# A state-space layer and a gated feed-forward on one core: a decay tile in place of a third transpose, and per-block bursts

## The chip, the core and the metric

One core of a Trainium2 chip runs the whole kernel. It has TensorE for matrix products (PE; its weight loads are a row of their own, PEld), VectorE (DVE), ScalarE (ACT), GpSimd (POOL) and a queue engine (SP) that issues most of the transfers. The metric is the device time of the program in microseconds, the median over runs. Three runs of the kernel before gave 408.99, 411.08 and 411.17 us.

## The reference

Two layers follow each other. The first is a state-space layer over batch 4, 8 heads, 768 steps, head size 32 and state size 16, in chunks; the second is a root-mean-square norm and a gated feed-forward over 3072 tokens, 256 channels and 1536 hidden units. The three weight matrices come as 64-bit floats.

```python
cum = np.cumsum(la, axis=-1)                       # la: log of a in the chunk
M = (Cc @ Bc^T) * exp(cum_i - cum_j) * causal      # per batch and head
y_intra = M @ xc
y_inter = (Cc @ state) * exp(cum_i)
state = exp(sum(la)) * state + sum_j Bc_j xc_j^T exp(cum_last - cum_j)
...
xn = x / sqrt(mean(x * x) + 1e-6) * rms_g          # x: y as 3072 x 256
g = xn @ w_gate
out = (g * sigmoid(g) * (xn @ w_val)) @ w_out
```

The chunk length is free in the result; the kernel uses its own.

## The kernel before

*Tiling.* Tokens are worked in six blocks of 512 (`TB`). A block has two pairs, a pair two chunks of 128 tokens (`P`); from pair 2 on each chunk is treated as two halves of 64 (`HC`), with a state each. Eight heads with 16 state rows fill 128 partitions; `NQ` is four groups of two heads, each on 32 partitions.

*The state-space part of a pair.* `load` and `load_x` bring B, C and x. `scale` (L478) makes on VectorE Cd = C times exp(cum), and Bd = B times the decay to the end of the half chunk. `turn` (L494) transposes B, C and Cd of one chunk on TensorE into a tile tp; `turned` (L502) copies the transposed B and Cd into the tile T, and `turned_of` (L509) copies the transposed C twice, each time masked to one head of every two. `products_at_once` (L546) is a burst of 32 small products: C B^T for all heads, into four PSUM banks called g. `decayed` and `decayed_one` (L552, L559) multiply them on VectorE by the decays L, in place. `outputs` (L644) is a burst of small products into four banks y: first the state's part (state times transposed Cd), then the intra part (x times the decayed L), and at its end `additions` (L574), the state additions of the next pair. `squares` and `taken_out` (L688, L705) bring y out, and `states` (L589) makes the new states.

The decays L of pairs 4 to 11 are made like this: `row_sums` and `row_store` (L1005, L1011) put sums of logs into the DRAM tile rowd; `spread` (L453) broadcasts them to 64 partitions each; `subtract`, `exponential` (L460, L467) take the token's own sum off, and apply the exponential and the causal mask (on POOL, L471).

*The feed-forward.* `product_gv` (L826) makes gate and value with seven products per group of two tiles of hidden units, and `taken_gv`, `total_gv`, `silu_gv`, `hide_gv` (L848 to L867) combine them on ScalarE and VectorE. `product_o` (L915) and its combinations do the same for the second matrix. Block 0 uses plain products (`products_early`, `products_gv`, `first_projection`), while the 64-bit weights are fetched and converted (`fetch`, `power`, `mantissa`, `weight`).

*Order.* The order of all steps is written out by hand in one string (`order`, L1114). A step such as `2:P.7.1` is product 7 of group 1 of block 2; `2:g.0` is the C B^T burst of the first pair of the block behind it. Each engine gets its instructions in the order of that string and runs them in that order; waits follow from tiles and buffers. Each transfer on SP waits in its place too.

*Buffers touched.* `raw` has three buffers each for B, C and x; `ssd` two for Cd, Bd, T and L. The banks of PSUM: two single ones (tag "one"), pair 2 for g and y, and four for gate and value. Each `bank` call takes one of the two single ones.

Of the kernel before, what the change touches and what calls it, by code (L numbers as in the profile page):

```python
# [9 lines left out]
FP32 = mybir.dt.float32  # L10
# [10 lines left out]
def kernel(  # L21
# [91 lines left out]
    def load(p, queues=(nc.sync, nc.sync)):  # L113
        b, c0 = divmod(2 * p, NC)
        br = raw.tile([P, 2, NH, N], FP32, tag="br", name="br")
        cr = raw.tile([P, 2, NH, N], FP32, tag="cr", name="cr")
        st.setdefault(p, {}).update(B=br, C=cr)
        for i in range(2):
            sl = slice((c0 + i) * P, (c0 + i + 1) * P)
            for dst, src in ((br, B), (cr, C)):  # L120
                queues[i].dma_start(out=dst[:, i], in_=src[b, :, sl, :].rearrange("h s n -> s h n"))

    def load_x(p, queue=nc.sync):
        b, c0 = divmod(2 * p, NC)
        st.setdefault(p, {})["x"] = raw.tile([P, 2, NH, D], FP32, tag="xr", name="xr")
        for i in range(2):
            sl = slice((c0 + i) * P, (c0 + i + 1) * P)
            queue.dma_start(out=st[p]["x"][:, i], in_=x[b, :, sl, :].rearrange("h s n -> s h n"))
# [284 lines left out]
    def pair_tile(g):  # L413
        p = g // 2
        if p not in Ls:
            Ls[p] = ssd.tile([P, 2, NH, P if p < 2 else HC], FP32, tag="L", name="L", bufs=2)
        return Ls[p][:, g % 2]
# [60 lines left out]
    def scale(p):  # L478
# [3 lines left out]
        for name, src, d in (("Cd", "C", to_i), ("Bd", "B", from_j)):  # L482
# [11 lines left out]
    def turn(p, i, parts=3):  # L494

        s = st[p]
        ps["t", p, i] = tp = bank("tp", (P, parts, P))
        for k, src in enumerate((s["B"], s["C"], s.get("Cd"))[0:parts]):
# [3 lines left out]
    def turned(p, i, copy):  # L502
        tp = ps["t", p, i]
        if tp.shape[1] == 3:
            copy(out=transposed(p)[:, i, 0::3], in_=tp[:, 0::2])
        else:
            copy(out=transposed(p)[:, i, 0], in_=tp[:, 0])

    def turned_of(p, i, t, scaled):  # L509

        scaled(transposed(p)[:, i, 1 + t], ps["t", p, i][:, 1], tmask[:, t:t + 1])
# [11 lines left out]
    def product(p, todo):  # L523
        T = st[p]["T"]
        for i in range(2):
            for q, g in todo:
# [8 lines left out]
                for u in halves:  # L535
                    nc.tensor.matmul(  # L536
                        out=g[u, P * i:P * i + P].rearrange("p (t m) -> p t m", t=2),
                        lhsT=T[r, i, 0, u], rhs=T[r, i, 1:3, u], start=(i == 0), stop=True,
# [7 lines left out]
    def products_at_once(p, g):  # L546
# [3 lines left out]
        product(p, [(0, g[:, 0]), (1, g[:, 1]), (2, g2), (3, g3)])  # L550

# [92 lines left out]
    def outputs(p, y):  # L644

        if p < 2:
            return first_outputs(p, y)
        s = st[p]
        ps["y pair", p] = y
        y = [y[:, 0], y[:, 1], bank("y2", (P, 512)), bank("y3", (P, 512))]  # L650
        ps["y", p] = y
        first = (2 * p) % NC == 0
        opened = set()

        def product_y(k, u, i, rows, **operands):
            nc.tensor.matmul(out=y[2 * k + u][rows, i * HC:(i + 1) * HC],  # L656
# [4 lines left out]
        for i in range(2):  # L661
            for u in range(2):
                for q in range(NQ):
                    if first and i == 0 and u == 0:
                        continue
                    r, o = slice(32 * q, 32 * q + 32), 64 * (q % 2)
                    S = state[2 * (2 * p + i) + u - 1]
                    product_y(q // 2, u, i, slice(o, o + 64),
                              lhsT=S[r].rearrange("p t d -> p (t d)"),
                              rhs=s["T"][r, i, 3, halves[u]], tile_position=(32 * q, o))  # L670
        opened |= {(k, u, o) for k, u, o_ in opened for o in (o_, o_ + 32)}
        for i in range(2):
            for h in range(NH):
                for u in range(2):
                    o = 32 * (h % 4)
                    product_y(h // 4, u, i, slice(o, o + 32), lhsT=s["x"][halves[u], i, h],
                              rhs=Ls[p][halves[u], i, h], tile_position=(HC * u, o))
        if 2 <= p < NPAIR - 1:
            additions(p + 1, [y[u][:, P:2 * P].rearrange("p (i t d) -> p i t d", i=2, t=2)
                              for u in range(2)])  # L680
        del st[p], Ls[p]

    def parts_of_y(p):
        y = ps["y", p]
        return [(0, slice(0, 2), ps["y pair", p][:, :, 0:P])] + [
            (1, slice(u, u + 1), y[2 + u][:, 0:P].unsqueeze(1)) for u in range(2)]

    def squares(p):  # L688
# [3 lines left out]
        tk = slice(half * 256, half * 256 + 256)  # L692
# [5 lines left out]
        sq2 = nrm.tile([P, 2, 2, 2, HC], FP32, tag="sq2", name="sq2", bufs=1)  # L698
        for k, us, y in parts_of_y(p):
            nc.scalar.activation(out=sq2[:, k, :, us].rearrange("p i u m -> p u i m"),  # L700
                                 in_=y.rearrange("p u (i m) -> p u i m", i=2), func=AF.Square)
        s2 = sq2.rearrange("p k i u m -> p k (i u m)")
        nc.gpsimd.tensor_tensor(out=sqs[blk][:, tk], in0=s2[:, 0], in1=s2[:, 1], op=ALU.add)

    def taken_out(p, copy):  # L705
# [3 lines left out]
        tk = slice(half * 256, half * 256 + 256)  # L709
# [5 lines left out]
        for k, us, y in parts_of_y(p):  # L715
            copy(out=yts[blk][:, k, tk].rearrange("p (i u m) -> p u i m", i=2, u=2)[:, us],
                 in_=y.rearrange("p u (i m) -> p u i m", i=2))
# [287 lines left out]
    def row_sums(k):  # L1005

        ps["row", k] = r_ps = bank("r_ps", (P, P))
        nc.tensor.matmul(out=r_ps, lhsT=laf[:, 2 * k * BH:(2 * k + 4) * BH], rhs=mid,
                         start=True, stop=True)

    def row_store(k):  # L1011
        c = 2 * k
        r_sb = nrm.tile([P, P], FP32, tag="r_sb", name="r_sb", bufs=2)
        nc.vector.tensor_copy(out=r_sb, in_=ps.pop(("row", k)))
        nc.sync.dma_start(out=rowd[:, c * BH:(c + 4) * BH].rearrange("u r m -> r u m"),
                          in_=r_sb.rearrange("r (u m) -> r u m", u=2))

# [14 lines left out]
    rowv = rowd.rearrange("u r m -> u (r m)")  # L1032
    def by_scalar(out, in_, scale):
        ac.activation(out=out, in_=in_, func=AF.Copy, scale=scale)

    def by_vector(out, in_, scale):
# [10 lines left out]
        "scale": scale, "turn": lambda p, i: turn(p, i, 3 if p > 1 else 2),  # L1047
        "T": lambda p, i: turned(p, i, ac.copy if p else dv.tensor_copy),
        "Tt": lambda p, i, t: turned_of(p, i, t, by_scalar if p else by_vector),
# [5 lines left out]
        "y": lambda p: outputs(p, take("y", ("y", p))),  # L1055
# [16 lines left out]
        "row": row_sums, "rowout": row_store,  # L1072
# [15 lines left out]
    def of_chunk(n, fn):  # L1088
# [9 lines left out]
        "turn": of_pair(1, turn), "T": of_pair(1, lambda p, i: turned(p, i, ac.copy)),  # L1098
        "Tt": of_pair(1, lambda p, i, t: turned_of(p, i, t, by_scalar)),
        "scale": of_pair(1, scale),  # L1100
        "g": of_pair(1, lambda p: products_at_once(p, pair_of_banks("g", 2))),
        "L": of_pair(1, lambda p: decayed(p, 0)),
        "L1": of_pair(1, decayed_one),
        "A": of_pair(1, additions), "S": of_pair(1, states),
        "y": of_pair(1, lambda p: outputs(p, pair_of_banks("y", 2))),
        "sq": of_pair(1, squares), "yt": of_pair(1, lambda p: taken_out(p, ac.copy)),
# [9 lines left out]
        0:gcol 0:never 0:after 0:fetch.2 0:mid 0:ident16 0:whole16 0:fetch.3 0:idle.7 0:mask.0.0/1  # L1116
        0:mask.0.1/0 0:hmask 0:part 0:part2 0:fetch.4 0:head 0:mids 0:fetch.5 0:bc.2 0:x.2 0:fetch.6
        0:aT 0:la0 0:log4.0.4 0:fetch.7 0:log 0:mask.1.1/2 0:log4.4.2 0:log4.6.2 0:sel 0:upto2
        0:after2 0:whole 0:r.0 0:tmask 0:parts.0 0:middles 0:c*2 0:turn.0.1 0:T.0.1 0:cx 0:kinks
        0:eps 0:Tt.0.1.0 0:d 0:dx 0:fetch.8 0:Tt.0.1.1 0:sums.0.1 0:exp.0.1 0:turn.0.0 0:Tt.0.0.0  # L1120
        0:T.0.0 0:Tt.0.0.1 0:scale.1 0:cc 0:sums.0.0 0:exp.0.0 0:mean 0:turn.1.0 0:never16 0:g.0.1/0
        0:L.0.1 0:turn.1.1 0:bc.3 0:T.1.1 0:Tt.1.0.1 0:Tt.1.1.1 0:Tt.1.0.0 0:T.1.0 0:Tt.1.1.0
        0:fetch.9 0:sums.1.1 0:exp.1.1 0:g.0.0/1 0:scale.0 0:last.0 0:Tl.0 0:L.0.0 0:pow.0 0:man.0
        0:A.0 0:S.0 0:bc.4 0:row.1 0:rowout.1 0:man.1 0:wt.0 0:g.1.1/0 0:A.1 0:S.1 0:last.1 0:pow.1
        0:L.1.1 0:Tl.1 0:pow.2 0:mask.1.0/2 0:sums.1.0 0:exp.1.0 0:row.0 0:g.1.0/1 0:mask.3/0
        0:pow.5 0:man.5 0:fetch.10 0:r.1 0:y.0/2 0:sq.0 0:pow.3 0:L.1.0 0:y.1/1 0:sq.1 0:wt.1
        0:scale.2 0:rowout.0 0:man.2 0:pow.6 0:yt.0 0:ydone.0 0:turn.2.0 0:early.0.0/2 0:parts.1
        0:sums.3 0:exp.3 0:ms.0 0:rs.0 0:wt.2 0:pow.4 0:yt.1 0:ydone.1 0:early.0.1 0:mask.2/0
        0:sums.2 0:turn.2.1 0:man.3 0:wt.5 0:wt.3 0:early.1.0/1 0:early.1.1 0:man.4 0:fetch.11
        0:man.6 0:fetch.14 0:scale.3 0:exp.2 0:pow.7 0:xn.0 0:wt.6 0:T.2.0 0:T.2.1 0:Tt.2.1.0  # L1130
        0:Tt.2.1.1 0:Tt.2.0.0 0:Tt.2.0.1 0:table.0 0:x.3 0:wt.4 0:gate.2/0 0:man.8 0:man.7
# [186 lines left out]
```

## Time and profile before

| | us |
|---|---|
| median of the three runs | 411.08 |
| the profiled execution, its own time | 409.49 |
| its span | 407.4 |
| last chain piece on TensorE ends, then a sum and a store of the result | 404.69 |

| stage (us of the span) | what runs |
|---|---|
| 0 to 26 | start: masks, sums of logs, pairs 0 and 1 |
| 26 to 94 | block 0's feed-forward, conversion of the weights, pairs 2 and 3 |
| 94 to 147 | block 1, pairs 4 and 5 |
| 147 to 390 | blocks 2 to 5, pairs 6 to 11 until 331 |
| 390 to 407 | last products of block 5, result out |

| group (line, engine, what) | count | us busy | mean ns |
|---|---|---|---|
| L499 PE, transposes of Cd | 20 | 5.5 | 273 |
| L536 PE, C B^T from pair 2 on | 320 | 6.9 | 280 |
| L656 PE, y from x and L | 640 | 8.6 | 224 |
| L656 PE, y from the state | 296 | 6.6 | 224 |
| L582 PE, state additions in a y burst | 264 | 5.1 | 226 |
| L484 DVE, Cd | 12 | 5.0 | 415 |
| L562 DVE, L by g, 256 columns | 20 | 8.0 | 418 |
| L556 DVE, L by g, 512 columns | 10 | 6.8 | 681 |
| L1034 ACT, masked copies of C | 44 | 14.0 | 379 |
| L505 ACT, copies of B and Cd | 20 | 7.4 | 372 |
| L703 POOL, sum of the squares | 10 | 7.7 | 766 |
| spread, rowd to L, 128 KB each | 32 | | 3.2 us to landing |
| row sums to rowd, 64 KB each | 2 | | 2.3 us to landing |

How to read it: busy time of a group is the time in which at least one of its instructions runs, so that overlapping small products have a busy time far below count times mean. A product in 32-bit floats is two records. What matters for the end is the distance between starts on TensorE, not the duration of a record: two full products of 256 columns start 216 ns apart, and last 381.

### The profile page before, as it was taken

The page shows a single profiled execution, that of the slowest core. Times are in us where ns is not written, and L with a number is a line of the kernel's source. Part 1 is how long each engine was busy: PE and PEld are TensorE (multiplying, and loading weights), DVE is VectorE, ACT ScalarE, POOL GpSimd, SP SyncE. Part 2 cuts the span into 40 slices and gives each one's busy share as a digit, 9 for nine tenths or more (in the row PEclk, how much of TensorE's full clock was granted, in tenths as well). Part 3 has the DMA queues.
Part 4 walks back from the last instruction along what each step waited for, and adds up shares of the span by engine and source line. Part 5 has one row for each costly group of instructions (what it writes and reads, how often), then busy time and mean ns, then how long its engine had stood idle before and what let it go on. Part 6 is the DMA issues. An engine that isn't in the chain of part 4 may idle for free.

```text
span 407.4 us, 9550 instructions
## 1 busy us (share of the span) xinstructions
PE 399.9 (98%) x3867; PEld 340.4 (84%) x3867; DVE 303.7 (75%) x698; ACT 231.9 (57%) x506; POOL 37.5 (9%) x61
## 2 busy tenths in 40 slices
PE   8999999999899999999999999999999999999997
PEld 4566577888688899888899988899988899988997
DVE  5999999898976787856799278779455777265863
ACT  3899989795556445664584355534566442453500
POOL 4010000003200001300023000001300000000000
PEclk9999999999999999999999999999999999999999
DMA  9998937400401171302080501020300000100001
GB/s 112 231 213 173 266 118 209 53 0 5 75 0 28 29 126 39 44 1 55 20 131 8 79 2 53 2 80 2 77 2 0 2 4 0 53 1 2 0 2 52
DMA packets 87371, 23.91 MB, mean 59 GB/s; under 512 B 76800, under 2 KB 81152, under 8 KB 87328
## 3 DMA queue, kind: packets, MB, share of 16 engines
q1 hardware_dynamic: 83168, 23.05, 26.9%
q10 hardware_dynamic: 4160, 0.26, 0.8%
q8 instruction: 30, 0.49, 0.5%
q14 instruction: 13, 0.11, 0.1%
HBM read 20.02 MB, written 3.28 MB: 57 GB/s over the span
## 4 chain that ended last, share of the span: by engine, by line
PE 90%; DVE 4%; ACT 3%; DMA 1%; issue 1%; SPq 0%; ACTq 0%
PE gate L844 27%; PE o L934 22%; PE val L844 20%; PE o L876 4%; PE gate L760 3%; PE y L656 3%; PE tp L499 2%; PE gate L770 2%; PE g L536 1%; PE ms L725 1%; DVE sw L814 1%; DVE s L907 1%; DMA L<-rowd 1%; PE e L422 1%; ACT e L183 1%
## 5 line engine op out<-in xcount | busy, mean ns | idle before, releaser
L856 DVE TENSOR_TENSOR c<-val,p 128x512 f32<-128x512 f32 x99 | 67.6, 688 | 46.3 <-PE val L844 27.5
L850 ACT COPY p<-gate 128x512 f32<-128x512 f32 x99 | 57.4, 586 | 52.4 <-PE gate L844 49.2
L844 PE MATMUL gate<-tx,sw 128*128 128x256 f32 x264 | 65.5, 381 | 0.0
L865 ACT ACTIVATE c<-c 128x256 f32<-128x256 f32 x99 | 39.9, 417 | 41.8 <-DVE c L856 41.6
L844 PEld LDWEIGHTS gate<-tx,sw 128*128 128x128 f32 x264 | 49.1, 190 | 7.0 <-ACT p L850 0.3
L869 DVE TENSOR_TENSOR h<-c 128x256 f32<-128x256 f32 x99 | 41.4, 433 | 17.4 <-ACT c L865 17.3
L844 PE MATMUL val<-tx,sw 128*128 128x256 f32 x132 | 33.9, 381 | 1.2 <-DVE c L856 1.2
L844 PE MATMUL val<-xn,wgv 128*128 128x256 f32 x132 | 34.1, 380 | 0.0
L844 PE MATMUL gate<-xn,wgv 128*128 128x256 f32 x132 | 34.0, 382 | 0.0
L844 PE MATMUL val<-xn,sw 128*128 128x256 f32 x132 | 33.9, 381 | 0.0
L844 PE MATMUL gate<-tx,wgv 128*128 128x256 f32 x132 | 33.8, 383 | 0.0
L471 POOL TENSOR_SCALAR_AFFINE_SELECT L<-L 64x512 f32<-64x512 f32 x32 | 23.5, 734 | 83.3 <-ACT L L469 72.9
L934 PEld LDWEIGHTS o<-two,s 128*128 128x128 f32 x240 | 28.3, 192 | 1.9 <-issue 1.4
L934 PE MATMUL o<-wo,h 128*128 128x128 f32 x240 | 29.5, 275 | 0.0
L934 PE MATMUL o<-two,s 128*128 128x128 f32 x240 | 29.3, 276 | 0.1
L934 PEld LDWEIGHTS o<-wo,h 128*128 128x128 f32 x240 | 28.4, 192 | 0.7 <-DVE h L869 0.2
L934 PE MATMUL o<-two,h 128*128 128x128 f32 x240 | 28.9, 275 | 0.0
L844 PEld LDWEIGHTS val<-tx,sw 128*128 128x128 f32 x132 | 24.7, 190 | 5.0 <-DVE c L856 1.6
L844 PEld LDWEIGHTS gate<-tx,wgv 128*128 128x128 f32 x132 | 24.4, 190 | 4.2 <-ACT p L850 0.6
L934 PEld LDWEIGHTS o<-two,h 128*128 128x128 f32 x240 | 27.8, 192 | 0.0
L844 PEld LDWEIGHTS val<-xn,wgv 128*128 128x128 f32 x132 | 24.5, 190 | 3.9 <-DVE c L856 0.6
L844 PEld LDWEIGHTS val<-xn,sw 128*128 128x128 f32 x132 | 24.6, 190 | 3.5 <-DVE h L869 0.2
(179 smaller groups left out, 645.9 us busy)
## 6 DMA issues: line engine op xcount, KB each, us to landing
L<-rowd SPq DMA_DIRECT2D x32, 128.0 KB, 3.2
xr<-in_x_dram SPq DMA_DIRECT2D x24, 128.0 KB, 4.2
wr<-in_moe_w_out_dram SPq DMA_DIRECT2D x6, 512.0 KB, 5.0
wr<-in_moe_w_gate_dram SPq DMA_DIRECT2D x5, 512.0 KB, 5.8
wr<-in_moe_w_val_dram SPq DMA_DIRECT2D x5, 512.0 KB, 5.9
out_dram<-ob SPq DMA_DIRECT2D x9, 256.0 KB, 2.2
br<-in_B_dram SPq DMA_DIRECT2D x22, 64.0 KB, 3.8
cr<-in_C_dram SPq DMA_DIRECT2D x22, 64.0 KB, 3.1
```

The lines of the kernel that those rows point to most:

```text
L471: nc.gpsimd.affine_select(out=L[r], in_=L[r], pattern=[[0, NH], [1, HC]], compare_op=ALU.is_ge, fill=0.0, base=0, channel_multiplier=-1)
L499: nc.tensor.transpose(out=tp[:, k], in_=src[:, i].rearrange("p h n -> p (h n)"), identity=ident)
L656: nc.tensor.matmul(out=y[2 * k + u][rows, i * HC:(i + 1) * HC], start=(k, u, rows.start) not in opened, stop=True, skip_group_check=True, ...
L760: nc.tensor.matmul(out=gv[:, k], lhsT=w[:, t, fs], rhs=xns[0][:, t], start=(t == 0), stop=(t == 1))
L770: nc.tensor.matmul(out=gv[:, k, tk], lhsT=w[:, t, fs], rhs=yts[0][:, t, tk], start=(s == 0 and t == 0), stop=(t == 1), skip_group_check=True)
L844: nc.tensor.matmul(out=dst[:, half[w]], lhsT=lhsT, rhs=rhs, start=(k in (1, 2, 5) and w == 0), stop=True, skip_group_check=True)
L850: nc.scalar.copy(out=t, in_=Xs[j])
L856: nc.vector.tensor_tensor(out=t, in0=Zs[j], in1=a, op=ALU.add)
L865: nc.scalar.activation(out=u, in_=src[:, half[0]], func=AF.Silu)
L869: nc.vector.tensor_tensor(out=hidden_tile(blk, j)[:, c // 10 - 1, c % 10 - 1], in0=u, in1=src[:, half[1]], op=ALU.mult)
L876: nc.tensor.matmul(out=o, lhsT=hs_[blk, f // 2][:, f % 2, k // 2, (k % 2) * P:(k % 2 + 1) * P], rhs=wo[:, f], start=opens, stop=(f == NF - ...
L934: nc.tensor.matmul(out=o[t] if apart else o[:, t * P:(t + 1) * P], lhsT=lhsT[:, t], rhs=rhs, start=(k in (1, 2, 4, 5) and j == 0 and (apar ...
```

## The change

- The transposes of Cd go for pairs 2 to 11 (`turn` makes B and C alone). `scale` makes only Bd there. In place of the transposed Cd, T gets the transposed C times a decay tile dT (`turned_decayed`, on VectorE out of PSUM).
- dT holds exp(cum) for each head, on that head's 16 partitions. `row_sums` gets a second product, with the matrix `upto`; `row_decays` applies the exponential and stores the rows into a new DRAM tile rowe; `spread_decays` broadcasts a pair's rows into dT (in the buffers of Cd).
- `turn`, `turned`, `turned_of` treat a pair at once, not a chunk at once, from pair 2 on.
- Blocks 2 to 5 (pairs 4 to 11): one burst of C B^T for both pairs, into g of full width (`products_of_block`); L is one tile for the block and multiplied in three instructions (`decayed_block`); one burst of outputs for both pairs, with the additions of both pairs of the next block at its end; squares and copies at double width, and the first square goes straight into sq.
- Buffers: B and C two instead of three, x four instead of three, r_sb three instead of two.
- The order is written anew throughout, the start included (places of fetches, loads, conversions, fillers).

```diff
-        br = raw.tile([P, 2, NH, N], FP32, tag="br", name="br")
+        br = raw.tile([P, 2, NH, N], FP32, tag="br", name="br", bufs=2)
...
+            Ls["of", p // 2] = L = ssd.tile([P, 4, NH, HC], FP32, tag="L", name="L", bufs=2)
...
-        for name, src, d in (("Cd", "C", to_i), ("Bd", "B", from_j)):
+        for name, src, d in (("Cd", "C", to_i), ("Bd", "B", from_j))[0 if p < 2 else 1:]:
...
+    def spread_decays(p):
+        b, c0 = divmod(2 * p, NC)
+        st.setdefault(p, {})["dT"] = d = ssd.tile([P, 2, P], FP32, tag="Cd", name="dT")
+        nc.sync.dma_start(
+            out=d.rearrange("p i m -> p (i m)"),
+            in_=rowe[b * NH:(b + 1) * NH, c0 * P:(c0 + 2) * P].unsqueeze(1).to_broadcast(
+                [NH, N, 2 * P]))
+
+    def turned_decayed(p):
+        nc.vector.tensor_tensor(out=transposed(p)[:, :, 3], in0=ps["t", p][:, 1], in1=st[p]["dT"],
+                                op=ALU.mult)
...
+    def products_of_block(blk, g):
+
+        ps["g", blk] = gs = [g[:, 0], g[:, 1], bank("g2", (P, 512)), bank("g3", (P, 512))]
+        ps["g pair", blk] = g
+        for k in range(2):
+            product(2 * blk + k, [(q, gs[q][:, 256 * k:256 * k + 256]) for q in range(NQ)], k == 0)
...
-        ps["row", k] = r_ps = bank("r_ps", (P, P))
-        nc.tensor.matmul(out=r_ps, lhsT=laf[:, 2 * k * BH:(2 * k + 4) * BH], rhs=mid,
-                         start=True, stop=True)
+        ps["row", k] = r_ps = bank("r_ps", (P, 2, P))
+        for j, rhs in enumerate((mid, upto)):
+            nc.tensor.matmul(out=r_ps[:, j], lhsT=laf[:, 2 * k * BH:(2 * k + 4) * BH], rhs=rhs,
+                             start=(j == 0), stop=True, skip_group_check=True)
...
+    def row_decays(k):
+        c = 2 * k
+        r_sb = nrm.tile([P, P], FP32, tag="r_sb", name="e_sb", bufs=3)
+        nc.scalar.activation(out=r_sb, in_=ps["row", k][:, 1], func=AF.Exp)
+        nc.sync.dma_start(out=rowe.rearrange("h (c m) -> c h m", m=P)[c:c + 4], in_=r_sb)
...
+        "y": when(1, lambda b: outputs([2 * b, 2 * b + 1], pair_of_banks("y", 2),
+                                       [2 * b + 2, 2 * b + 3] if b + 1 < NBLK else [])),
```

Of the order, the stretch in which pair 2 is made ready, before and after:

```diff
-        0:scale.2 0:rowout.0 0:man.2 0:pow.6 0:yt.0 0:ydone.0 0:turn.2.0 0:early.0.0/2 0:parts.1
-        0:sums.3 0:exp.3 0:ms.0 0:rs.0 0:wt.2 0:pow.4 0:yt.1 0:ydone.1 0:early.0.1 0:mask.2/0
...
+        0:last.1 0:Tl.0 0:y.0/1 0:r.1 0:man.5 0:pow.3 0:mask.2/2 0:Tl.1 0:y.1/0 0:parts.1 0:sums.2
+        0:sq.0 0:yt.0 0:ydone.0 0:early.0.0/1 0:pow.5 0:wt.5 0:fetch.16 0:man.3 0:sq.1 0:yt.1
+        0:ydone.1 0:ms.0 0:mask.3/0 0:wt.3 0:pow.4 0:exp.2 0:rs.0 0:man.4 0:fetch.9 0:scale.2
+        0:row.0 0:rowout.0 0:rowe.0 0:dT.2 0:man.6 0:dT.3 0:xn.0 0:sums.3 0:exp.3 0:table.0 0:wt.4
+        0:pow.7 0:early.0.1 0:norm.0 0:tx.0 0:early.1.0/2 0:early.1.1 0:norm.1 0:silu.0 0:hid.0
+        0:bc.3 0:man.7 0:fetch.12 0:turn.2 0:T.2 0:Tt.2.1 0:Tt.2.0 0:Td.2 0:wt.7 0:pow.6 0:fetch.10
```

In these steps man, pow and wt are parts of the conversion of a weight piece, yt copies y, ms and rs belong to the norm, early is block 0's gate and value product before the norm, and Td is the multiplication with dT.

## The prediction

> **What bounds the kernel now.** I read the page first, then the busy time by stage, then the chain of waits, then the groups of instructions by shape, and last the timeline where the chain leaves TensorE.
>
> ```profile
> span 407.4 us, 9550 instructions
> PE 399.9 (98%) x3867; PEld 340.4 (84%) x3867; DVE 303.7 (75%) x698; ACT 231.9 (57%) x506; POOL 37.5 (9%) x61
> ```
>
> TensorE is the first suspect, but a busy share is an average. By stage (columns: the stretch and its length, then busy time and count of PE, PEld, DVE, ACT, POOL, the granted clock, the DMA share and GB/s):
>
> ```profile
> 0.00:22.00 22.00, 19.57 (x175) 11.71 (x179) 16.82 (x60) 13.84 (x29) 4.93 (x17) 1.00 1.07 170
> 22.00:50.00 28.00, 27.04 (x290) 16.55 (x283) 27.51 (x60) 26.21 (x43) 1.46 (x2) 1.00 0.92 217
> 50.00:80.00 30.00, 29.95 (x390) 23.20 (x389) 28.22 (x65) 25.22 (x56) 1.46 (x2) 1.00 0.57 140
> 80.00:112.00 32.00, 30.77 (x172) 26.27 (x171) 28.96 (x58) 22.85 (x44) 6.06 (x8) 1.00 0.14 25
> 224.00:268.00 44.00, 44.00 (x507) 37.85 (x506) 28.12 (x65) 21.95 (x58) 1.63 (x2) 1.00 0.19 39
> ```
>
> There are two regimes. Up to 112 us VectorE is as full as TensorE (27.51 of 28 us), because it converts the weights. From 112 us on TensorE never rests and VectorE has a third of its time free. There, what TensorE doesn't have to do comes off the end. The chain of waits (start, length, what) prices its small work:
>
> ```profile
> 134.97 0.86 PE val L844 x4
> 135.84 0.62 PE g L536 x32
> 136.46 1.06 PE gate L844 x4
> 137.52 0.86 PE val L844 x4
> ...
> 148.75 0.33 PE tp L499 x3
> ```
>
> Four products last 0.86 us. Those behind the burst g of C B^T last 1.06: leaving a burst costs something that its own 0.62 us does not contain. Three transposes are 0.33, so 0.109 each, with no such surcharge.
>
> **What the Trainium skill says.** "TensorEngine Tiling (Array Packing)", Tiling Modes, says that a change of the tiling mode drains the array. The trace agrees with a number: single starts around the g burst at 167.6 us stand 310 ns after the last full product's (216 is usual), then come four groups of eight at 0, 160, 269 and 378 ns, then the next full product 244 ns after the last group, and the one behind it 320 ns later. "Advanced Engine Details and Errata" says that GpSimd and two-port VectorE work block each other on a shared port. The timeline agrees for additions of two SBUF operands: the same shape doubles when POOL starts.
>
> ```profile
> 97.95 0.42 DVE L814 TENSOR_TENSOR sw<-wgv 128x256 f32<-128x256 f32 x1
> 98.17 6.51 POOL L471 TENSOR_SCALAR_AFFINE_SELECT L<-L 64x512 f32<-64x512 f32 x8 [33.84 <-ACT L L469]
> 98.29 0.87 DVE L814 TENSOR_TENSOR sw<-wgv,sw 128x256 f32<-128x256 f32 x1
> ```
>
> "DMA: Bandwidth & Descriptors" puts about 2 us of fixed cost on a transfer, mostly its receipt; here a 64 KB store to DRAM took 2.3 us and a 128 KB broadcast from it 3.2.
>
> **The change part by part** (against the profiled execution, 409.49 us with a span of 407.4; the median of the runs shown is 411.08).
>
> *Third transpose.* Pairs 2 to 11 lose two transposes of Cd each: 20 x 0.109 = 2.18 us of TensorE. On VectorE the scaling of C (0.415) becomes a multiplication of the transposed C with the decay tile out of PSUM. No row shows it; the nearest (L562, PSUM by SBUF into SBUF, 128x256) is 0.418. Even, and with one SBUF operand instead of two it should suffer less from POOL. ScalarE does one copy (0.372) instead of two and two masked copies of 256 columns (nearest 0.381) instead of four at 0.379, so 1.1 us less per pair; off the path, worth nothing by itself. New: two matrix products for the row sums, 2 x 2 passes x 0.109 = 0.44 us of TensorE, two exponentials (about 0.29 each), two stores and ten broadcasts of 128 KB.
>
> *One burst of C B^T for each of blocks 2 to 5.* A burst of 32 costs, from the full product before it to the second behind it, 135.84 to 137.52 less the usual 0.86, that is 0.62 + 0.20 = 0.82 us. Its four groups are worth 4 x 0.109 = 0.436, so the fixed part is 0.38 us, which four mergers save: 1.54 us.
>
> *One burst of outputs for each of these blocks.* By single starts, the fixed part is 0.093 in, 0.029 for the first group, 0.109 more where the shape changes from state products (32x64) to intra products (64x32), 0.130 out and 0.104 at the second product behind: 0.465 us, four times, 1.86 us. The products and state additions themselves stay in number (640, 296, 264 records plus 24 outside). Between these bounds I take the full 1.86; nothing would be saved if the drain grew with the burst, which no row excludes.
>
> TensorE in sum: -2.18 - 1.54 - 1.86 + 0.44 = -5.14 us. Nearly all of it lies after 112 us, uncovered by anything.
>
> *Mergers on the other engines.* Six multiplications by L per block (two at 0.681, four at 0.418) become three at double width (1.22 + 2 x 0.681), 3.03 us to about 2.6; squares and copies of y about 1.2 us less ScalarE per block. Off the path.
>
> *The new order, first part.* I counted both orders, instruction by instruction with the durations of the rows. Before, the first early gate product waits for 20.3 us of VectorE work and starts at 26.18 us, with 13.8 us of TensorE work behind it. Now the row parts of pair 2 (four operations, 1.7 us) come before yt, so TensorE waits with 13.3 us done for 20.5 us of VectorE work, and the early product comes after 21.3. VectorE's lead over TensorE there goes from 6.5 to 7.2 us, and at 44 to 60 us of TensorE work from about 1 to 5 us up to about 4 to 5.5. A lead becomes a stall only beyond what VectorE's own waits gave before. I take +0.5 us; the bounds are -1 and +2.
>
> *The new order, later part.* TensorE stood 1.39 us at 106.28: the chain goes from a copy p over eleven microseconds of VectorE work, with POOL slowing it, to the next value product; and 0.24 us at 216. In the new order the same stretch has sub, cw and two spread further between the products and more than 1.5 us of TensorE work to spare at each VectorE wait; I take -1.0 (bounds -1.6 and 0). Elsewhere after 112 us the tightest covers are alike: a copy and a sum with at least 0.87 us of product time behind them, as before. For waits that I don't see I add 0.6 (bounds 0 and 3).
>
> *Queues.* On SP, bc.2 now waits for scale.0 (two buffers instead of three), and what stands behind it (stores of the row sums, x.4) waits too; the first user is 10 us of TensorE work away. A decay tile can only be issued after the product that read its buffer two pairs earlier; the spreads behind it in SP's queue have 9 us or more of work before their readers. Cover enough for 3.2 to 4.2 us of transfer; if it were gone, VectorE would stop in order.
>
> The sum: -5.1 + 0.5 - 1.0 + 0.6 = -5.0 us. The profiled execution would go from 409.5 to 404.5, the median from 411.08 to 406.1; I say 406.0.
>
> **The rivals.**
>
> *The saving is eaten in the first 112 us.* For it: VectorE is at 98% from 22 to 50 us and its lead grows by up to 3.6 us in the new order; also the drain could grow with the burst, which is the case that the change doesn't do what it says: then only -2.18 + 0.44 remain of TensorE, -1.7. Against it: the later part is TensorE's alone, and bursts at L844 have the same surcharge whether 73 or 81 products are in them. With +2 in the first part, no recovery of the 1.39 and +2 of new waits, -5.1 + 4 = -1: 410 us.
>
> *Slower, by the decay tile's round trip.* Exponential, store to DRAM, broadcast back, and then an in-order multiplication on VectorE, with the weights' conversion queued behind it: wt.7, wt.6, man.8, and for them TensorE's gate products. Place: the tile of pair 2, in the stage with DMA at 92%. Between row sums and the multiplication VectorE has 0.28 + 1.1 + 1.2 + 0.68 + 1.36 + 1.7 + 1.36 + 0.68 + 1.1, about 9.5 us; the path needs 0.3 + 2.3 + 3.2, 5.8 us, or 8.5 with the 5.9 us of the full stage's weight loads. From 9.5 us on each microsecond stops VectorE; the change becomes slower than before when this, with the later tiles, costs over 5 us, so at a trip of some 15 us. Priced at 8 us lost: 414 us. Against it: no transfer on the page takes over 6 us.
>
> **How the numbers follow.** Forecast 0.70, with 402.5 to 409 as its own range; eaten 0.16; slower 0.14. The bounds of the forecast's terms added up in full give -7.7 to -0.1 us (403.4 to 411.0); the range goes 1.4 us lower, since the runs before themselves lie 2.2 us apart, and up to 411, where half of the eaten case is in. A measurement of this kernel tells about 0.5%, 2 us, from no change: faster is below 409.0, slower above 413.1. The forecast puts nearly all of its 0.70 into faster; the eaten case splits into 0.02 and 0.14; with a little of the forecast the same comes to 0.15, slower 0.14.
>
> **What would show it.** Right: no Cd row at the transposes, four g bursts of 64 in blocks 2 to 5 at about 1.06 us in the chain, four y bursts with one surcharge each, and from 112 us on a stretch shorter by over 4 us. The first early gate product at 26 to 27 us. Wrong: a chain through a decay tile or its store; VectorE waiting on DMA between 30 and 45 us; more than 2 us of TensorE gaps after 112 us; a g burst of 64 at over 1.3 us.

## The result, and the profile after

| | before | after |
|---|---|---|
| median on one chip, us | 410.16 (408.99 to 411.17) | 415.87 (415.49 to 416.37) |
| profiled execution, us | 409.49 | 415.65 |
| its span, us | 407.4 | 413.9 |
| granted TensorE clock, mean | 1.000 | 0.975 |

The ratio of after to before is 1.0141, with a 95% interval of 1.0104 to 1.0178: slower by 5.7 us, where 5 us less were forecast. (Here and below a median is over all executions of a kernel, and a ratio leaves out those over 1.5% above its fastest.) The page of after, its head and two rows of the span in 40 slices of 10.3 us:

```profile
span 413.9 us, 9466 instructions
...
PE 404.9 (98%) x3855; PEld 345.5 (83%) x3855; DVE 302.8 (73%) x686; ACT 222.4 (54%) x452; POOL 36.9 (9%) x57
...
PE   7899999999999989999999999999999999999997
...
PEclk9659999999999999999999999999999999999999
```

TensorE has 5 us more busy time with 12 records fewer, and the row of the granted clock has a 6 and a 5 where before had nines throughout. The same stages as in the prediction (stretch and length, then busy time and count of PE, PEld, DVE, ACT, POOL, the granted clock, DMA share, GB/s):

```profile
0.00:22.00 22.00, 18.69 (x117) 11.02 (x117) 13.50 (x52) 9.80 (x21) 4.87 (x17) 0.78 1.05 194
22.00:50.00 28.00, 28.00 (x299) 18.22 (x296) 23.71 (x47) 22.16 (x38) 1.51 (x2) 0.81 0.62 141
50.00:80.00 30.00, 29.77 (x417) 19.86 (x416) 28.09 (x70) 25.23 (x53) 1.53 (x2) 1.00 0.84 188
80.00:112.00 32.00, 32.00 (x150) 28.15 (x150) 27.89 (x61) 23.51 (x39) 1.75 (x2) 1.00 0.23 43
```

In the first 22 us TensorE ran 117 products where it had run 175, at a mean clock of 0.78. From 22 to 50 us it is full, and VectorE, which had been busy for 27.51 us, has 4 us to spare: the limit has changed sides. Two pieces of the chain of waits in the start of before, then that of after (start, length, what):

```profile
8.46 0.90 PE d_ps L379 x4
...
26.18 1.97 PE gate L770 x8
```

```profile
10.94 0.92 PE d_ps L380 x4
...
16.86 2.01 PE g L556 x8
18.86 1.15 PE r_ps L1060 x4
...
28.96 1.87 PE y L678 x32
...
33.64 1.01 PE y L678 x32
...
35.54 1.92 PE gate L821 x8
```

Thirty-two output products of one line last 1.87 us at 28.96 and 1.01 at 33.64; between the two, at 32.92 us, the clock came back (below). The first early gate product, which started at 26.18 us before, starts at 35.54, 9.4 us later. From there to the end of the span it is 378.4 us, against 381.2 before. So the later part did get shorter, by 2.8 us (5.5 were forecast), and the start lost over three times as much. Both halves have to be explained.

### The profile page after: what moved, and what is told of

It is laid out like the page before. It is cut to its first block, busy times and chain, and to the rows that moved or that the text cites. A ratio compares the mean times of both kernels' runs of the same rounds, so it can differ in the third digit from the quotient of the medians.

```text
span 413.9 us, 9466 instructions
## 1 busy us (share of the span) xinstructions
PE 404.9 (98%) x3855; PEld 345.5 (83%) x3855; DVE 302.8 (73%) x686; ACT 222.4 (54%) x452; POOL 36.9 (9%) x57
## 3 DMA queue, kind: packets, MB, share of 16 engines
HBM read 21.33 MB, written 3.41 MB: 60 GB/s over the span
## 4 chain that ended last, share of the span: by engine, by line
PE 88%; DVE 7%; DMA 2%; issue 1%; ACT 1%; SPq 1%; DVEq 0%
PE gate L895 26%; PE o L985 22%; PE val L895 20%; PE o L927 5%; PE y L697 3%; PE g L556 2%; PE gate L821 2%; PE gate L811 2%; PE g L563 1%; PE ms L776 1%; DMA xr<-in_x_dram 1%; PE tp L506 1%; DVE S L652 1%; DMA br<-in_B_dram 1%; DVE wgv L202 1%
```

## Experiments on the start

What the clock does is exact in the trace, which records its changes. Two rows of stretches of after, the 3.4 us just before the clock fell and all the time at the lower clock, then the row of before for the same place:

```profile
9.02:12.44 3.42, 1.66 (x18) 0.99 (x15) 3.04 (x9) 1.32 (x2) 0.69 (x1) 1.00 1.16 213
12.44:32.92 20.48, 20.23 (x152) 11.77 (x152) 12.26 (x27) 12.60 (x28) 0.72 (x1) 0.50 0.86 226
```

```profile
9.17:12.59 3.42, 3.29 (x38) 1.92 (x36) 2.31 (x8) 2.54 (x3) 0.55 (x1) 1.00 1.26 226
```

TensorE was busy for 1.66 of 3.42 us, then ran at 0.50 for 20.48 us. In before it was busy for 3.29 us there. Why was it empty? VectorE's timeline of after there (start, busy time, line, operation; in brackets the idle time before it):

```profile
8.80 0.17 DVE L341 MEMSET mean<- 128x128 f32 x1
8.88 1.08 DVE L290 CAST never<-never 64x64 bf16<-64x64 f32 x2
9.97 0.29 DVE L519 COPY T<-tp 128x128 f32<-128x128 f32 x1
```

Two casts of 64x64, which make the tile never16, took 1.08 us; in before they took 0.33, at 12.69 us. Here they stand beside GpSimd's multiplication `early`, from 8.63 to 9.71 us. The new order had put them there, ahead of the copy of T, though never16's first reader is far behind. The copy was a microsecond late, and the products d, which since the new order stand behind the second turn and want the PSUM bank that this copy and the two masked copies behind it give back, came at 10.94 us instead of 8.46.

Two theories followed: *clock* (TensorE's empty stretch lowered its clock, and the clock cost the 9 us) and *order* (the start is simply late in the new order). The first experiment moves the casts alone:

```diff
-        0:r.0*3 0:tmask 0:parts.0 0:middles 0:c*3 0:turn.0.1 0:cx 0:kinks 0:eps 0:mean 0:never16
+        0:r.0*3 0:tmask 0:parts.0 0:middles 0:c*3 0:turn.0.1 0:cx 0:kinks 0:eps 0:mean
...
-        0:A.0 0:S.0 0:man.1 0:g.0.1/2 0:L.0.1 0:pow.0 0:wt.0 0:row.1 0:rowout.1 0:turn.1.0
+        0:A.0 0:S.0 0:man.1 0:g.0.1/2 0:L.0.1 0:never16 0:pow.0 0:wt.0 0:row.1 0:rowout.1 0:turn.1.0
```

> The changed kernel with one VectorE instruction pair moved: the two 64x64 casts of never16 (0.54 us each in time, 1.08 us together, while GpSimd works on early at 8.63 to 9.71 us) go behind L.0.1. Theory clock: the changed kernel is slower because TensorE is busy for only 0.45 of the 3.41 us up to 12.44 us and so runs at half clock until 32.92 us. The copy of T then starts at about 8.9 us instead of 9.97, the C decay products at about 9.9 instead of 10.94, the busy share of that stretch rises to about 0.75, the clock stays at 1.00, the first early gate product comes at 26 to 28 us and the time is 406 to 409 us. Theory order: the start is late because its loads and steps come late in the new order, at any clock. Then only the 1.1 us is won: first early gate product at about 34.5 us, time about 414.8 us.

Measured: 407.23 us (406.13 to 409.64, 20 runs), 0.9947 of before, interval 0.9933 to 0.9961. The span is 404.7 us, and the profile has:

```profile
PEclk9999999999999999999999999999999999999999
```

```profile
8.91 0.23 DVE L519 COPY T<-tp 128x128 f32<-128x128 f32 x1
...
16.50 0.38 DVE L290 CAST never<-never 64x64 bf16<-64x64 f32 x2
```

```profile
26.79 1.97 PE gate L821 x8
```

(Its row of the clock, VectorE's timeline, the chain.) Moving two casts took 9.2 us off the span (413.9 to 404.7). At their new place they last 0.38 us. The early product is where the prediction had it, at 26 to 27 us. Theory order falls. (Four of the 20 executions show a clock of 0.996 and took 408.8 to 409.6 us; they were not profiled. One stretch of 3.41 us at 0.50 would give 0.996, an estimate.)

The second experiment puts the same hole into the kernel before, which has nothing else of the change:

```diff
-        0:eps 0:Tt.0.1.0 0:d 0:dx 0:fetch.8 0:Tt.0.1.1 0:sums.0.1 0:exp.0.1 0:turn.0.0 0:Tt.0.0.0
+        0:eps 0:never16 0:T.0.1 0:Tt.0.1.0 0:turn.0.0 0:fetch.8 0:Tt.0.1.1 0:d 0:dx 0:sums.0.1 0:exp.0.1 0:Tt.0.0.0
```

(0:T.0.1 and 0:never16 are taken from where they stood.)

> The kernel before with the same hole put in: never16's casts and the second turn ahead of d, as the changed kernel has them. Nothing else of the change is in it. Theory clock: the clock falls to 0.50 for some 20 us from about 12.5 us on (granted mean about 0.975), the first early gate product moves from 26.2 to 31 to 35 us, and the time is 415 to 419 us. Theory order: only the hole itself is paid, 0.5 to 1.5 us: 410.5 to 412 us, clock 1.00.

Measured: 417.95, 417.64 and 417.85 us at a granted clock of 0.975, as theory clock expected, and one execution of 410.84 at 1.00. The 23 executions of before beside it all had 0.999 or more. Busy time and clock of the profiled one:

```profile
8.40:11.81 3.41, 1.35 (x9) 0.88 (x10) 3.10 (x13) 0.00 (x0) 1.24 (x2) 1.00 1.22 204
11.81:32.29 20.48, 20.48 (x158) 11.93 (x158) 13.06 (x30) 12.92 (x25) 0.00 (x0) 0.50 0.87 205
```

Again 20.48 us at half clock after a stretch with 1.35 of 3.41 us busy, and the early product came at 34.8 us. One program, two times 7 us apart, and the clock tells them apart: the execution that kept it paid only 1.3 us for the hole, over the 409.56 of before beside it. That is the loss of after without the rest of after.

One objection stays: in both, VectorE's delay and TensorE's hole went together. The third experiment leaves the casts early in the changed kernel and fills the hole with products on zeros:

```diff
+    def still(p, half, n):
+        for k in range(n):
+            nc.tensor.matmul(out=ps["e", p, half][:, 0, 0:256], lhsT=warm[:, 0:P], rhs=warm,
+                             start=False, stop=False, skip_group_check=True)
...
-        0:fetch.11 0:fetch.7 0:fetch.8 0:T.0.1 0:Tt.0.0.1 0:turn.0.0 0:sums.0.1 0:Tt.0.1.1 0:cc 0:d
+        0:fetch.11 0:fetch.7 0:fetch.8 0:T.0.1 0:Tt.0.0.1 0:turn.0.0 0:sums.0.1 0:Tt.0.1.1 0:cc 0:still.0.0.6
+        0:d 0:still.0.0.4
```

> The changed kernel with never16's casts left where they are, and TensorE's hole filled: six products of 128x128x256 on zeros ahead of d and four behind it, added onto a PSUM tile that they leave as it is. VectorE is as late as in the changed kernel. Theory clock (an idle TensorE is what costs): clock 1.00, first early gate product at 27 to 29 us, time 407.5 to 409.5 us. Theory late VectorE (the held cast delays T, d and all that follows, and the clock only reports it): the time stays at 414 to 416 us, or the ten fillers cost another 1 to 2 us.

Measured: 407.89 us (407.50 to 408.41, 9 runs), ratio 0.9950, interval 0.9935 to 0.9965. The early product, by the chain:

```profile
28.07 1.96 PE gate L826 x8
```

The casts still take 1.13 us beside GpSimd, and the clock stays at 1.00. Ten products that compute nothing took 8 us off. The cause is shown: TensorE's idleness, by way of its clock. The late VectorE and the ten products cost 1.3 us together (28.07 against 26.79).

A fourth kernel is cast_late with d ahead of the second turn, as in before, and that turn behind sums.0.1:

```diff
-        0:fetch.11 0:fetch.7 0:fetch.8 0:T.0.1 0:Tt.0.0.1 0:turn.0.0 0:sums.0.1 0:Tt.0.1.1 0:cc 0:d
+        0:fetch.11 0:fetch.7 0:fetch.8 0:d 0:T.0.1 0:Tt.0.0.1 0:sums.0.1 0:turn.0.0 0:Tt.0.1.1 0:cc
```

> As cast_late, and the products d of the decay at the chunk ends go ahead of the second turn, into the PSUM bank that is free by then, and the second turn behind sums.0.1. Theory clock: TensorE is busy for over 0.85 of 9 to 12.4 us, clock 1.00, first early gate product at 26 to 27 us, time 405.5 to 408 us, that is the changed kernel's own 378.4 us behind the early product and 26 to 27 us ahead of it, with 1.8 us around the span. Theory order: first early gate product at 33 to 34.5 us, time 413 to 415 us.

Measured: 406.66 us, ratio 0.9922 (0.9892 to 0.9952); early product at 26.77 us, where 26 to 27 was expected. But the busy share was not what I expected: the wait moved from d to the third turn, and from 8.0 to 11.4 us TensorE is busy for 0.71 of the time (the lowest share over any 3.41 us of the start is 0.74 in cast_late, 0.72 in before). One of its four executions took 414.04 us at a clock of 0.979; it was not profiled, so what share it had is not known. None of cast_late's 20 executions fell for so long, so its later d is the safer order. Where the edge lies, the share of 0.71 does not say: the recorded changes of the clock stand whole multiples of 3.413 us apart, and of the profiled stretches on that grid 0.49 and 0.40 lost the clock, while 0.64 in before (from 104.75 us) and 0.50 in fetch_mended (a later run, from 263.24 us) kept it:

```profile
263.24:266.65 3.41, 1.71 (x8) 1.18 (x7) 3.23 (x13) 0.38 (x1) 0.00 (x0) 1.00 0.03 7
```

## Experiments on the rest

After the early product 2.8 us were saved instead of 5.5. In cast_late it is 404.7 - 26.8 = 377.9 us, so 3.3. The chain of after around the first merged burst of outputs:

```profile
140.86 1.14 PE g L563 x61
142.00 1.06 PE val L895 x4
143.06 1.73 PE gate L895 x8
144.78 0.86 PE val L895 x4
145.65 2.43 PE y L697 x154
148.08 1.06 issue
149.14 0.38 PE y L697 x21
```

"issue" is time in which TensorE waited for nothing that the profile shows. The third burst, the last with a next block's additions behind it, shows the same:

```profile
266.12 1.97 PE y L697 x122
268.10 0.73 issue
268.83 0.62 PE y L697 x39
```

The second has it too (at 210.65). The stops are at different products, so no input explains them. I counted TensorE's instructions in the trace up to each stop (weight loads, products and semaphore operations):

```
kernel            stop ends at   between two starts   count   over a multiple of 256
after             149.14 us      1.28 us              2753    193
                  210.65         0.30                 4032    192
                  268.83         0.95                 5312    192
cast_late         140.51         1.28                 2753    193
                  259.62         0.65                 5312    192
```

(0.012 us is usual between two such starts.) The Trainium skill, "Runtime: NRT & Kernel Launch", Instruction fetch mechanics, says that instructions are fetched in blocks of 16 KiB, 256 instructions, and that the cost at a block's end is mostly hidden. The spacing agrees: all stops are at one place of a block of 256. Hidden it is not here. hole_filled, whose fillers put 20 instructions more ahead of the burst, stops at the count 2753 as well (1.59 us, until 141.87), 20 instructions earlier in the burst. A product in 32-bit floats is four instructions (two weight loads, two passes), a merged burst with its additions some 510, so two block ends fall into it. Before, a burst has about 240, at most 256. Without its stop the block before each of after's three would have been used up in 1.6 to 1.7 us; the quickest of the kernel before lasted 2.07.

To test it, start_mended's count was shifted by 110:

```diff
-        0:gcol 0:never 0:after 0:fetch.2 0:mid 0:ident16 0:whole16 0:fetch.3 0:idle.7 0:mask.0.0/2
+        0:gcol 0:never 0:after 0:fetch.2 0:mid 0:ident16 0:whole16 0:fetch.3 0:idle.2 0:mask.0.0/2
...
+        for k in range(60):
+            nc.tensor.matmul(out=ps["idle"][:, 0:32], lhsT=warm[0:32, 0:P], rhs=warm[0:32, 0:32],
+                             start=True, stop=True, tile_position=(0, 0))
```

> start_mended with 110 more TensorE instructions at the start: 60 products of 32x32x128 on zeros in place of five idle ones of 128x128x256, about the same 1.2 to 1.6 us, all of it in the time before the first transposes of inputs. Theory fetch: TensorE's stops inside three of the merged y bursts (at 148.08, 210.56 and 268.10 us in the changed kernel, 1.06, 0.09 and 0.73 us) lie where the count of TensorE instructions is 192, 192 and 193 over a multiple of 256, so they wait for a block of instructions, when two block ends fall into one burst. With the count shifted by 110 each burst holds one such end only; all three stops go, the time is 1.5 to 2.2 us below start_mended. Theory data: the products wait for L or S; then the stops stay at the same products, 0.5 to 1.2 us each, and the time is within 0.4 us of start_mended's.

Measured: 417.32 us (414.94 to 420.43), 1.0191 of before (1.0135 to 1.0248). The time went the wrong way, and I had the lengths wrong: I had reckoned the burst without its additions, and with them it holds two ends at this count as well. The five stops take 9.8 us together, and the early product comes 2.6 us later (29.39): the 60 small products took 1.77 us, and products after them last longer than in start_mended (1.40 us instead of 0.82 for four of full_ps); the trace's first record of the clock at 1.00 stands at 10.08 us there, at 4.92 in start_mended. But the places are the test, and they moved as the count says:

```
kernel            stop ends at   between two starts   count   over a multiple of 256
mended_shift       68.80 us      1.81 us              1729    193
                  145.54         1.67                 3009    193
                  208.78         2.04                 4288    192
                  268.22         2.55                 5568    192
                  336.88         1.73                 6849    193
```

Three of the five are now in the state additions, one behind a burst, one in the outputs of the last block. The one at 268 us was long enough to cost the clock as well: 3.41 us at 0.50 follow it.

```profile
265.89 2.33 issue
268.22 0.43 PE y L631 x23
268.66 1.16 PE gate L898 x4
269.81 3.32 PE val L898 x8
273.13 0.86 PE gate L898 x4
```

Eight products in 3.32 us are twice the 1.73 of the chain above. Theory data (waits for L or S) falls: it had the stops stay at the same products.

Next, tail_mended moved two VectorE steps for the wait of 0.72 us at 284 us. fetch_mended also put the state additions behind 3 to 4 us of other products, as a step Ay of their own, and shifted the count by 72 (here the first of three blocks):

```diff
-        3:ex.0 4:dT.0 4:Tt.0.1 4:Td.0 3:s4.1 4:dT.1 3:s4.5 3:ex.3 3:ex.2 3:Otake.7 3:Oadd.22
-        3:Oadd.21 3:Oadd.11 4:P.1.1 4:take.1.1 3:O.3.0 4:P.1.0 4:take.1.0 4:P.2.1 4:C.11.1
+        3:ex.0 4:dT.0 4:Tt.0.1 3:s4.1 4:dT.1 3:ex.3 3:ex.2 3:Otake.7 3:Oadd.22
+        3:Oadd.21 3:Oadd.11 3:s4.5 4:Td.0 4:P.1.1 4:take.1.1 3:O.3.0 4:P.1.0 4:take.1.0 4:P.2.1 4:C.11.1
...
-        2:x.0 2:S.0 2:S.1 1:sq 1:two.2 1:O.1.0 1:O.5.0 1:s2.0 2:dT.1 1:O.4.0 1:s3.5 1:O.1.1 1:O.1.2
-        1:O.1.3 1:O.1.4 1:O.1.5 1:O.2.0 1:O.2.1 1:O.2.2 1:O.2.3 1:O.2.4 1:O.2.5 1:O.5.1 1:O.5.2
+        2:x.0 1:sq 1:two.2 1:O.1.0 1:O.5.0 1:s2.0 2:dT.1 1:O.4.0 1:s3.5 1:O.1.1 1:O.1.2
+        1:O.1.3 1:Ay 2:S.0 2:S.1 1:O.1.4 1:O.1.5 1:O.2.0 1:O.2.1 1:O.2.2 1:O.2.3 1:O.2.4 1:O.2.5 1:O.5.1 1:O.5.2
```

> start_mended with two VectorE steps moved in the fourth block: s4.5 and the decayed transposes Td.0 of the next block behind the three additions Oadd. TensorE's wait of 0.72 us at 284.0 us is for a bank that Oadd.11 gives back, 1.0 us of VectorE work (0.41 + 0.66) ahead of it goes. If so the wait falls to under 0.2 us and the time is 0.5 to 0.8 us below start_mended (about 405.6 us beside 406.3). Rival: the three additions themselves come late because o is late, and the wait stays within 0.2 us of 0.72.

Measured: 407.60 us (406.01 to 414.58, 7 runs), ratio 0.9917 (0.9888 to 0.9946). The wait fell from 0.72 to 0.38 us, by 0.34 where over 0.5 was expected, so neither the expectation nor its rival holds; TensorE still waits for the additions, which run from 283.62 to 284.69 us. In three of the seven executions the clock was 0.975 to 0.979 (the start is that of start_mended), so the median says nothing of a change of 0.3 us.

> tail_mended with the state additions of the next block put 3 to 4 us behind the burst of outputs instead of in it, and 72 more TensorE instructions at the start (39 products of 32x32x128 in place of three idle ones). Worked out from the order of the instructions, with a block of 256 instructions that can't be used up in less than 2.9 to 3.4 us: one stop of 1.1 to 1.6 us is left (at 139 us) of three, and three returns from other products to the additions cost about 0.25 us each. Theory fetch: the stops at 200 and 257 us are gone, the one at 139 us stays or grows, time within 0.7 us of tail_mended either way. Theory data: all stops are at the products where they were.

Measured: 408.96 us (408.25 to 409.87), ratio 0.9976 (0.9964 to 0.9987). No stop is left in the bursts: at 139 us, where one was expected, a block used up in 1.70 us passed, so the 2.9 to 3.4 us of the expectation are no bound. One of 0.43 us is in the additions at 262.45 us, count 5568, 192 over. The time did not follow, and lies outside the 0.7 us expected around tail_mended: the early product comes 1.4 us later (27.89 instead of 26.53; the 39 small products took 1.22 us where three idle ones take about 0.7), and at 266.42 us TensorE waits 1.86 us for an addition c, in front of which VectorE now had the state updates of the moved step:

```profile
264.85 0.91 DVE L655 SCALAR_TENSOR_TENSOR S<-S,fcol,A 128x64 f32<-128x64 f32 x3
265.68 1.28 DVE L915 TENSOR_TENSOR c<-val,p 128x512 f32<-128x512 f32 x2
266.42 0.73 PEld L903 LDWEIGHTS val<-xn,sw 128*128 128x128 f32 x4 [2.10 <-DVE c L915]
```

The last pair, both on cast_late's start, with those updates behind the additions c, tells the two parts of the edit apart. What the second of them, adds_late_shift, has beyond the first:

```diff
-        0:gcol 0:never 0:after 0:fetch.2 0:mid 0:ident16 0:whole16 0:fetch.3 0:idle.7 0:mask.0.0/2
+        0:gcol 0:never 0:after 0:fetch.2 0:mid 0:ident16 0:whole16 0:fetch.3 0:idle.2 0:mask.0.0/2
...
+        for k in range(38):
+            nc.tensor.matmul(out=ps["idle"][:, 0:32], lhsT=warm[0:32, 0:P], rhs=warm[0:32, 0:32],
+                             start=True, stop=True, tile_position=(0, 0))
...
-        0:exp.0.1 0:T.0.0 0:Tt.0.0.0 0:Tt.0.1.0 0:turn.1.1 0:dx 0:scale.0 0:bc.2 0:sums.0.0
+        0:still.0.0.3 0:exp.0.1 0:T.0.0 0:Tt.0.0.0 0:Tt.0.1.0 0:turn.1.1 0:dx 0:scale.0 0:bc.2 0:sums.0.0
```

> cast_late with the state additions of the next block 3 to 4 us behind the merged burst of outputs in the three inner blocks, and in the fourth block s4.1, s4.5 and Td.0 on VectorE behind the three additions Oadd. The count of TensorE instructions ahead of the bursts is that of the changed kernel. Theory fetch: the stops inside the bursts stay at the count 192 over a multiple of 256, on the products of C with L, at about 140, 201 and 259 us, 0.3 to 1.3 us each; only the wait at 284 us shrinks, from 0.72 to under 0.4 us. Time within 0.8 us of cast_late (406.4 to 407.2 us). Rival, length of the burst: a burst without the additions is short enough, the stops go though nothing was shifted, and the time is 1 to 2 us below cast_late.

> adds_late with 72 more TensorE instructions at the start (38 products of 32x32x128 and three of 128x128x256 on zeros in place of five idle ones). Theory fetch: the stops at 140, 201 and 259 us go, as in fetch_mended, and this time no wait of 1.9 us at 266 us comes in their place, since the next block's state updates on VectorE stand behind the additions to c. Time 404.5 to 405.8 us, 1 to 2 us below adds_late. Rival: the stops are as in adds_late and the time within 0.4 us of it.

Measured: adds_late 407.45 us (407.05 to 408.71; 0.25 above its range), 0.9943 (0.9924 to 0.9962); adds_late_shift 406.33 us (405.56 to 407.11), 0.9909 (0.9888 to 0.9930). The first burst of outputs in adds_late, then in adds_late_shift, by their chains:

```profile
138.98 0.93 PE y L697 x57
139.90 1.34 issue
141.24 0.43 PE y L697 x25
141.67 2.87 PE o L990 x24
```

```profile
138.99 1.96 PE y L705 x132
140.95 2.87 PE o L998 x24
```

adds_late keeps all three stops, 1.55, 0.88 and 0.95 us at the counts 2753, 4033 and 5313. With 72 instructions more at the start there is none in the bursts; one of 0.76 us is left among the output projection's products of the last block (until 328.13, count 6849). So the count decides, not the length of the burst, and the rival falls. From the early product to the start of TensorE's last the profiled execution of the one takes 376.5 us, of the other 373.7; 0.9 of these 2.8 us are given back at the start, where the early product comes at 28.15 instead of 27.22. By the medians the gain is 1.1 us, within the 1 to 2 expected, but 406.33 lies above the 404.5 to 405.8 expected. adds_late_shift is 3.3 us faster than before's 409.68 beside it. That is not the change alone, since steps on VectorE were moved as well; with only the hole mended (cast_late) the change is worth 2.3 us.

The traces record the fetches too. The page of after has, among its DMA queues (packets, MB, share):

```profile
q8 instruction: 30, 0.49, 0.5%
```

These are 30 packets of 16,384 bytes, spread over the span, and TensorE's 7,778 recorded instructions are 30.4 times 256 (31 packets for the 7,888 of mended_shift; no other engine has 1,000 instructions). Taken in order, one packet for each block, which is an assignment of mine that no trace contradicts:

```
kernel             packet starts   ends     block used from   packet's start to use
after              146.73 us       147.84   149.14 us         2.42 us   stop
                   207.84          209.07   210.65            2.81      stop
                   266.23          267.52   268.83            2.60      stop
mended_shift       265.86          266.79   268.22            2.36      stop
adds_late          138.83          139.78   141.24            2.41      stop
adds_late_shift    135.62          136.84   140.09            4.47      none
before, quickest   243.70          244.63   248.74            5.04      none
```

In all eleven traces no block is used sooner than 2.2 us after its packet starts, and each stop named here ends 2.2 to 2.9 us after it. With this assignment the stops are waits for instructions. The speed at which a block is used up is only half of it: the one of 1.70 us before 140.09 in adds_late_shift passed without a stop, since the next block's packet had started 2.7 us before it began. In mended_shift, before 268.22, that packet started 1.55 us after the block began, and the stop is the longest of all. What sets the start of a packet is not shown.

## Why the prediction was wrong

**The step that failed** is "The new order, first part": "I take +0.5 us; the bounds are -1 and +2." It measured +9.4. The count of work ahead of the early product was good: with the casts moved it comes at 26.79 us, so +0.6. What failed was its premise. I priced every row at its duration in before, where the clock is 1.00 in all five stretches, and treated that column as a constant. It was 0.50 for 20.48 us of after's start. Nor did I ask what the new place of the two casts would cost beside GpSimd, though the shared port stood in my own text. The bounds were bounds on waiting; the real cost was in the speed of the work that didn't wait.

**The rivals.** "The saving is eaten in the first 112 us" had the place and neither the mechanism nor the size: VectorE was not the limit there, it had 4 us to spare. The decay tile's round trip played no part: the trace has no wait of VectorE ahead of any of the ten multiplications by it, and TensorE waits for one of their results once, 0.2 us. Its price, 414 us, lies near the 415.87 measured by chance.

Two readings of the stages were too wide, without weight for the result: in the first 22 us VectorE had 16.82 us of work beside TensorE's 19.57, and behind 112 us TensorE rested for the 0.24 us at 216 that the prediction names itself.

**TensorE's terms**, us from start to start, from the first early product to the last product:

```
                                           before   after    change
transposes (57 and 40 records)               6.28    4.37    -1.91
row sums and token sums                      0.43    0.87    +0.44
gate and value products                    219.32  216.76    -2.56
state additions                              4.41    3.88    -0.53
C B^T                                        6.22    6.06    -0.16
outputs y                                   12.48   15.07    +2.59
output projection                           94.30   94.17    -0.13
other (masks, their sums, means and so on)  34.77   34.01    -0.76
all                                        378.21  375.19    -3.02
```

Transposes (-2.18 forecast, of which three records lie ahead of this stretch) are as forecast. That the row of the sums has the +0.44 forecast is chance: all of before's row sums lie ahead of the stretch (16.0 to 19.4 us), so its 0.43 is for two records of token sums alone, and after has half of its row sums inside. Most of the -0.76 is no saving either: of the mask sums 38 records lie in the stretch instead of 74, and the other 36 ahead of it. The two merger terms, -1.54 and -1.86, can't be read from the rows of g and y, since a surcharge falls on the products behind the burst. With the 1.39 us gap taken out of the gate and value row (-1.17), the stops out of y (1.27 + 0.29 + 0.94 = 2.50, leaving +0.09), and 0.24 us of waiting before and 0.94 after out of the projection (-0.83), these rows with those of C B^T and the state additions give -1.17 - 0.53 - 0.16 + 0.09 - 0.83 = -2.6 us instead of -3.4: by this reckoning right in kind, and a quarter of it did not come. A burst of 64 took 1.14 us in the chain (1.06 forecast).

**The later part** (-1.0): the 1.39 us gap is gone, as expected. In place of the 0.24 at 216 there is 0.22 at 214.65 us, a block end too (count 4288, 192 over; packet 2.42 us before), and a new wait of 0.72 ends at 293.48.

**Waits not seen** (+0.6, bounds 0 and 3): 2.5 us of instruction stops, inside the bounds. The mechanism was in none of my lists. I asked whether the drain grew with the burst; what grew was the number of instructions in it, so that a whole block was used up within one burst, in 1.6 to 1.7 us, before the next had come.

## What to carry to other kernels

Read the granted clock as a quantity that a change can move: before moving anything into an engine's wait, add up TensorE's busy time over each 3.4 us of the start (0.49 of one was too little here), and if a new order makes a hole, fill it with products on zeros or move the one instruction that makes it. When bursts of small products are merged, count instructions and not only products, look where the blocks of 256 end, and compare the starts of the packets on the instruction queue with them. A cheap instruction that nobody needs yet is not free ahead of one that TensorE waits for.

## What the runs showed of the hardware

- The clock. The Trainium skill, "TensorE: Matmul & The Clock Gate", Part 1, says that the clock falls after an idle window of about 3.4 us and rises after a busy one. The recorded stretches agree with the window: 3.41 and 20.48 us, one and six of 3.413. The rest differs: it fell with TensorE busy for 0.49 (after) and 0.40 (before_gap) of a window, no gap being longer than 2.1 us, and it came back after six windows although TensorE was busy for 20.23 of the 20.48 us. Why six there and one in mended_shift stays open, and so does the exact edge: 0.50 kept the clock in fetch_mended, and the executions of start_mended and tail_mended that lost it were not profiled.
- The stops at block ends are shown by their place, by shifts of 20, 72 and 110 instructions, and by the packets: a block could be used 2.2 to 2.9 us after its packet started, 1.2 to 1.7 us after it ended. In the blocks named here a packet started between 2.8 us before and 1.8 us after the block ahead of its own began; the cause of that stays open.
- Two casts of 64x64 took 1.08 us beside a GpSimd multiplication and 0.33 to 0.38 without one. In the page's chain nothing shows this, since no semaphore is waited for: the chain of after led through the load of x there.
